# Row DFT one pass later, rows normalised further ahead, nine tiles transposed by DMA, and a new order of the first loads

## The chip, the cores and the metric

The kernel runs on one core of a Trainium2 chip. The metric is the device time of one execution in microseconds (us). One execution was also recorded by the hardware profiler, and the lines shown below come from that record. "SP", "ACT" and "POOL" queues are the DMA queues that these engines issue into; DVE is VectorE, PE is TensorE.

## The reference, cut to what matters

```
xn = layernorm(x, over D)                      # x: 1 x 2048 x 576, bf16
s  = irfft2(rfft2(xn, axes (S, D)) * (w_r + i w_i))
z  = gelu(xn @ w_in)                           # 2048 x 4608
z1, z2 = z[:, :2304], layernorm(z[:, 2304:])
g  = (w_sp @ z2 + b_sp) * z1                   # w_sp: 2048 x 2048
out = x + s * silu(g @ w_out)
```

Every step after the first needs xn, in the 2048 x 576 form with the 576 columns on the partitions (`xnT`): both the row DFT of `rfft2` and the product with `w_in` contract over the columns.

## The kernel before, in words

The 2048 rows are 16 tiles of 128 rows (`MT = 16`, index `m`). The 576 columns are padded to five blocks of 128 (`KS = 5`): four full ones (a row is folded about its middle) and one block that holds the 64 columns left over, each twice.

**The opening stage** goes over the 16 tiles. For a tile, `ln1_stats` and `ln1_aggr` take mean and variance on DVE, `rstd_of` makes the reciprocal deviation on POOL (tile 0: a square root on ACT and a reciprocal on DVE), `ln1_apply` (L293, L296, DVE) writes the normalised row tile into one of three buffers `XN[m % 3]`, `xpose` (L304) transposes its five blocks on PE into PSUM, and ACT copies the result to `xnT` (L305). `p0_fold` (L311, L312, DVE) adds and subtracts the halves, `p0` and `p0_tail` (L329, L321, PE) multiply by the DFT constants `CDSD`, `p0_out` (L334) copies the result on ACT and writes it to the DRAM tensor `Ad` from the POOL queue.

**The chunks** are the other PE work: a `Z2Chunk` (L458) is 128 rows times 384 columns of the second half of `w_in` (five matmuls, the last over 64 partitions), a `Z1Chunk` (L554) 128 columns of the first half times 512 rows. There are 96 of the first and 72 of the second kind; the string `kinds` fixes their order and `fill(n)` puts the next n between the DFT steps, wherever the code calls it. `z2_order` fixes the order of the `Z2Chunk`s: the first eight are tiles 0 to 3 with column chunks 0 and 1, the next eight the same tiles with chunks 2 and 3, the third eight with 4 and 5, and from the 25th on a tile has all its six chunks in a row. Each chunk is evicted by a gelu on ACT (L477, L471, L563), and its statistics are taken on DVE when a running estimate of the load (`spend`, `z2_stats`) leaves room.

PE, DVE and SP follow the order of the code exactly (a manual schedule); ACT and POOL are ordered by the framework. In the loop over `m` from 2, iteration `m` does `p0_fold(m)`, `ln1(m + 3)`, `ln1_apply(m + 2)`, two `fill`s and `p0(m)`; the transposes stand one or two tiles ahead.

**The later stages**: `p1`, `p2`/`p3`, `p4`, `p5` are the other passes of the Fourier filter, with chunks between them; `p1_read` (L342) reads `Ad` back when all tiles are written. The last stage (`main`, from 203 us on) multiplies by `w_sp`: seven products of half size (`prod`, L617) per unit in place of eight, with sums of `Z2` blocks (`tsum`, L601 to L605, DVE) and sums of `w_sp` slabs (`slab_sums`, L540, DVE) as operands. `w_sp` is loaded by DMA transposes (`load_slab`, L534).

**Loads**: each of the DMAs from the SP and ACT queues takes one of eight semaphores in turn, and waits for the DMA that had it eight transfers earlier. So SP, which issues nearly all loads, runs at most about eight transfers ahead.

Of the kernel before, what the change touches and what calls it, by code (L numbers as in the profile page):

```python
# [10 lines left out]
ACT = mybir.ActivationFunctionType  # L11
ALU = mybir.AluOpType
BF16 = mybir.dt.bfloat16
F32 = mybir.dt.float32
P = 128
# [75 lines left out]
def kernel(  # L91
# [135 lines left out]
    HT = H2 - 2 * P  # L227
    wv = B_w_in.rearrange("(a d) f -> a d f", a=2)

    def load_win_main(t, fs, eng=nc.sync):  # L230
        for a in range(2):
            eng.dma_start(out=t[:, a:KS - 1:2, :], in_=wv[a, 0:2 * P, fs].rearrange("(b p) f -> p b f", p=P))

    def load_win_tail(t, fs):
        for q in range(4):
            nc.sync.dma_start(out=t[q * HT:(q + 1) * HT, KS - 1, :], in_=wv[q % 2, 2 * P:H2, fs])

    def load_win(t, fs):
        load_win_main(t, fs)
# [5 lines left out]
        load_win(wb, fs)  # L245

    nc.scalar.dma_start(out=ident[:], in_=cd_id.ap())
    for m0, m1 in ((0, 1), (1, 2), (2, 4)):
        nc.sync.dma_start(out=XC[0][:, m0:m1, :], in_=xv[:, m0:m1, :])
    for n in range(2):  # L250
        load_win_main(WIN2[:, :, n * ZC:(n + 1) * ZC], slice(Fh + n * ZC, Fh + (n + 1) * ZC), nc.scalar)
    for g in range(3):
        (load_win if g else load_win_tail)(WIN2[:, :, 2 * g * ZC:2 * (g + 1) * ZC], slice(Fh + 2 * g * ZC, Fh + 2 * (g + 1) * ZC))
        if g == 0:
            nc.sync.dma_start(out=CDSD, in_=cd_cdsd.ap().rearrange("p (a k l) -> p a k l", a=2, k=3))
        load_x(g + 1)
    nc.sync.dma_start(out=G1, in_=cd_g1.ap().rearrange("p (s k) -> p s k", s=N2))

    def rstd_of(mv, n, tag):
        ve = small.tile([P, n], F32, tag=tag + "v")  # L260
        nc.gpsimd.tensor_scalar(out=ve[:], in0=mv[:, :, 1], scalar1=1e-5, scalar2=one[:, 0:1], op0=ALU.add, op1=ALU.mult)
        rs = small.tile([P, n], F32, tag=tag + "r", bufs=5)
        nc.gpsimd.tensor_tensor(out=rs[:], in0=ve[:], in1=mhalf[:, 0:n], op=ALU.pow)
        return rs
# [7 lines left out]
    def ln1_aggr(m):  # L272
        mv = small.tile([P, 1, 2], F32, tag="mv1", bufs=5, name="mv1")
        nc.vector.bn_aggr(out=mv[:, 0, :], in_=st1[m][:])
        if m == 0:
            rs = small.tile([P, 1], F32, tag="l11r", bufs=5, name="rs1")
            nc.scalar.activation(out=rs[:], in_=mv[:, :, 1], func=ACT.Sqrt, bias=eps[:], scale=1.0)
        else:
            rs = rstd_of(mv, 1, "l11")
        ln1_of[m] = (mv[:, 0, 0:1], rs[:, 0:1])  # L280

    def ln1(m):
        ln1_stats(m)
        ln1_aggr(m)

    st1 = {}
    ln1_of = {}

    def ln1_apply(m):
        xn = XN[m % 3]  # L290
        mean, rs = ln1_of[m]
        xr = XC[m // 4][:, m % 4, :].rearrange("p (a d) -> p a d", a=2)
        nc.vector.tensor_scalar(out=xn[:, 0:4 * P].rearrange("p (b a i) -> p a b i", b=2, a=2),  # L293
                                in0=xr[:, :, 0:2 * P].rearrange("p a (b i) -> p a b i", b=2), scalar1=mean, scalar2=rs,
                                op0=ALU.subtract, op1=ALU.mult)
        nc.vector.tensor_scalar(out=xn[:, 4 * P:KS * P].rearrange("p (r a i) -> p r a i", r=2, a=2),  # L296
                                in0=xr[:, None, :, 2 * P:H2].to_broadcast((P, 2, 2, HT)), scalar1=mean, scalar2=rs,
                                op0=ALU.subtract, op1=ALU.mult)

    def xpose(m):  # L300
        xn = XN[m % 3]
        pt = psh.tile([P, KS, P], BF16, tag="h")
        for ks in range(KS):
            nc.tensor.transpose(pt[:, ks, :], xn[:, ks * P:(ks + 1) * P], ident[:])  # L304
        nc.scalar.activation(out=xnT[:, m, :, :], in_=pt[:], func=ACT.Identity)  # L305

    Adw = Ad[:].rearrange("(c m p) l -> m p c l", c=2, p=P)

    def p0_fold(m):
        xe, xo = xnT[:, m, 0:KS - 1:2, :], xnT[:, m, 1:KS - 1:2, :]  # L310
        nc.vector.tensor_tensor(out=FS[m % 4][:, 0, :, :], in0=xe, in1=xo, op=ALU.add)  # L311
        nc.vector.tensor_tensor(out=FS[m % 4][:, 1, :, :], in0=xe, in1=xo, op=ALU.subtract)  # L312
# [19 lines left out]
    def p0_out(m):  # L332
        sg = PST[m % 8].rearrange("p (c l) -> p c l", c=2)
        nc.scalar.activation(out=sg.rearrange("p c (l a) -> p a c l", a=2),  # L334
                             in_=p0_ps[m][:, :, 0:2 * LE].rearrange("p a (c l) -> p a c l", c=2), func=ACT.Identity)
        nc.gpsimd.dma_start(out=Adw[m], in_=sg[:, :, 0:L])

    rowv = lambda t: t[:].rearrange("(p s) l -> p (s l)", s=N2)
    colv = lambda t: t[:].rearrange("(h p) l -> p h l", p=P)
# [354 lines left out]
    zq = iter(range(MT * NZC))  # L694
    yq = iter(range(FT * 4))
    tick = [0]
    kinds = "2" * 32 + "221" * 11 + "21" * 20 + "221" * 9 + "2111" * 4
    kinds += "2" * (MT * NZC - kinds.count("2")) + "1" * (FT * 4 - kinds.count("1"))
    held = []
    place = [0]  # L700
# [8 lines left out]
    def fill(n, lead=1.2, tails=None, ahead=None):  # L709
        for _ in range(n):  # L710
            i = place[0]
            place[0] += 1
            if i % 4 < 2:
                held.append(chunk(i))
                full(held[-1], True)
            if i % 4 == 1:
                if ahead:
                    ahead()
                done = held[:]
                held[:] = [chunk(i + 1), chunk(i + 2)]  # L720
                assert not tails or n == 1
                for r, c in enumerate(sorted(done + held, key=lambda c: c.wide)):
                    c.mm(KS - 1, slice(r % 2 * KT, (r % 2 + 1) * KT), c in held, c in done)
                if tails:
                    tails()
            elif i % 4 >= 2:
                done = [held.pop(0)]
                full(done[0], False)
            else:
                done = []  # L730
            for c in done:
                if c.wide == ZC:
                    z1_store(None, None)
                tick[0] += 1
                c.post()
            spend(0.82 if kinds[i] == "2" else 1.07)
            z2_stats(lead)

    SP, PE, DVE = mybir.EngineType.SP, mybir.EngineType.PE, mybir.EngineType.DVE
    with tc.manual_schedule(engines={SP, PE, DVE}):  # L740
# [4 lines left out]
        def keep_warm(n):  # L745
            pw = psh.tile([P, 512], F32, tag="h", name="pw")
            for i in range(n):
                nc.tensor.matmul(pw[:], lhsT=warm[:, 0:P], rhs=warm, start=True, stop=True)
# [3 lines left out]
        def p0_pair(m):  # L752
            p0_tail(m, False)
            p0_tail(m + 1, True)
            p0_out(m)

        ln1(0)
        ln1_stats(1, (0,))
        nc.vector.reciprocal(out=ln1_of[0][1], in_=ln1_of[0][1])
        ln1_apply(0)  # L760
        nc.scalar.activation(out=THF[:, 0:1], in_=ln1_of[0][1], func=ACT.Gelu_apprx_tanh)
        xpose(0)
        ln1_stats(1, (1,))
        ln1_aggr(1)
        keep_warm(2)
        fill(1, 0)
        ln1(2)
        ln1_apply(1)
        p0_fold(0)
        ln1_apply(2)  # L770
        ln1(3)
        fill(1, 0, lambda: p0_pair(0), lambda: (xpose(1), p0(0, True), xpose(2)))
        p0_fold(1)
        ln1_apply(3)
        p0(1, False)
        p0_out(1)
        ln1(4)
        fill(1, 0)
        fill(1, 0)
        nc.sync.dma_start(out=MM, in_=cd_mm.ap().rearrange("p (a k) -> p a k", a=3))  # L780
        for m in range(2, MT):
            if m % 2 == 0:
                xpose(m + 1)
            spend(0.78, 2.35 if m + 3 < MT else 0.6)
            p0_fold(m)
            if m + 3 < MT:
                ln1(m + 3)
            if m + 2 < MT:
                ln1_apply(m + 2)
            if m % 2 == 0:  # L790
                fill(1, 0)
                fill(1, 0, lambda: p0_pair(m), lambda: p0(m, True))
            else:
                p0(m, False)
                p0_out(m)
                fill(1, 0)
                if m + 1 < MT:
                    xpose(m + 1)
                fill(1, 0)
            if m in (6, 9):  # L800
                load_win1(m // 9)
        for ch in range(4):
            p1_read(ch)
        load_w(0)
# [15 lines left out]
        for hh in range(0, N2, 2):  # L820
            fill(2)
            if hh + 2 < N2:
                p2(hh + 2)
                spend(0.25, 1.5)
            if hh % 8 != 6:
                fill(1)
            p3(hh)
            spend(0.5)
# [26 lines left out]
        load_z1(0)  # L855
        tick[0] += 4
        z2_stats(99)
        for w in (0, 2, 1):
            tsum(0, w)
        later.append(partial(slab_sums, 2, 0, 2))  # L860
        assert place[0] > kinds.rindex("2")
        nc.sync.dma_start(out=BB, in_=B_b_sp.rearrange("(a s) -> a s", a=1).to_broadcast((P, S)))
# [2 lines left out]
            slab_sums(i, 0, 1)  # L865
        fill(len(kinds) - place[0])
        z1_store(None, None)
        assert not stats_q and not norm_q
        for i in range(2):
            slab_sums(i, 0, 2)  # L870
# [49 lines left out]
```

## Time and profile before

| | |
|---|---|
| median of 7 runs | 499.93 us (499.62 to 500.75) |
| the profiled execution, its own time | 500.48 us |
| its span in the profile | 498.7 us |
| PE busy | 487.8 us, 98% of the span |
| DVE, ACT, POOL busy | 341.0, 169.4, 207.6 us |
| PE clock granted | 1.00 throughout |
| opening stage, from the first transposes to its last row DFT | 5.6 to 48.5 us |
| first `p1` matmul | 59.36 us |
| first product of `main` | 202.82 us |

A line of instructions reads: line of the code, engine, operation, output and input, number, then busy time and mean duration, and then the time that the engine was idle just before and what it waited for. Matmuls are pipelined: a single one is given with some 0.33 us, but eight 128x384 matmuls in a row take 1.30 us in the chain of waits, and five transposes 0.28 us. The working below goes by these.

### The profile page before, as it was taken

To read this page: it belongs to the slowest core of one execution; us is meant where nothing else is said; L and a number is where in the kernel's file an instruction comes from. 1 tells how busy PE (TensorE), PEld (TensorE's weight loads), DVE (VectorE), ACT (ScalarE), POOL (GpSimd) and SP (SyncE) were. 2 spreads that over 40 slices of the span, in tenths; PEclk is the share of its full clock that TensorE was granted. 3 is DMA by queue.
4 is the path that set the end of the run, shared out by engine and by line. 5 is a ranking of instruction groups with operands and counts; after the bars stand their busy time and mean duration, and the time that the engine had idled before them with its cause. 6 is when DMAs were issued, how large, how long until landed. Compare 5 with 4: busy or idle time off the path is not lost.

```text
span 498.7 us, 9373 instructions
## 1 busy us (share of the span) xinstructions
PE 487.8 (98%) x3454; PEld 309.2 (62%) x3454; DVE 341.0 (68%) x747; ACT 169.4 (34%) x355; POOL 207.6 (42%) x280
## 2 busy tenths in 40 slices
PE   6999999999999999899999999999999999999996
PEld 2666454555556544466666677666666678888885
DVE  5776588898656797965565648856666547877634
ACT  4878777686878656200000011100000011000001
POOL 2664223444242684435535400455354311666500
PEclk9999999999999999999999999999999999999999
DMA  7971778988362999672111599021111753111202
GB/s 228 320 209 50 251 264 261 320 228 219 127 248 84 247 222 274 190 249 64 33 46 50 124 165 220 27 61 34 49 47 33 174 135 99 50 45 46 77 27 70
DMA packets 86766, 70.67 MB, mean 142 GB/s; under 512 B 39776, under 2 KB 79328, under 8 KB 86464
## 3 DMA queue, kind: packets, MB, share of 16 engines
q1 hardware_dynamic: 80480, 55.54, 42.3%
q0 software_dynamic: 5008, 13.71, 8.2%
q10 hardware_dynamic: 1232, 0.82, 0.6%
q8 instruction: 27, 0.44, 0.4%
q14 instruction: 19, 0.16, 0.1%
HBM read 40.40 MB, written 21.26 MB: 124 GB/s over the span
## 4 chain that ended last, share of the span: by engine, by line
PE 88%; DVE 3%; ACT 3%; DMA 2%; issue 1%; SPq 0%; POOL 0%; DVEq 0%; ACTq 0%
PE pm L617 43%; PE po L671 13%; PE ph L458 13%; PE ph L554 12%; PE pb L386 2%; PE pa L329 1%; DMA AR<-in_A_x_dram 1%; PE pa L374 1%; PE pa L428 1%; ACT Z L471 1%; DMA AR<-c_cdsd 1%; PE pa L350 1%; PE pa L402 1%; ACT Z L477 1%; PE pt L304 1%
## 5 line engine op out<-in xcount | busy, mean ns | idle before, releaser
L617 PE MATMUL pm<-AR,Z 128*128 128x384 bf16 (+1 forms) x864 | 138.8, 308 | 0.0
L621 DVE TENSOR_TENSOR AR<-pm,AR 128x384 f32<-128x384 f32 (+3 forms) x162 | 82.4, 512 | 70.8 <-PE pm L617 67.0
L617 PEld LDWEIGHTS <-Z 128*128 128x128 bf16 x864 | 84.5, 98 | 40.5
L617 PE MATMUL pm<-AR 128*128 128x384 bf16 (+1 forms) x648 | 107.0, 308 | 2.0 <-DVE AR L540 1.9
L458 PE MATMUL ph<-AR 128*128 128x384 bf16 (+1 forms) x480 | 89.6, 327 | 1.7 <-ACT AR L305 0.9
L554 PE MATMUL ph<-AR 128*128 128x512 bf16 (+1 forms) x360 | 85.9, 379 | 0.0
L617 PEld LDWEIGHTS <-AR 128*128 128x128 bf16 x648 | 63.3, 98 | 32.8 <-DVE AR L540 2.2
L631 ACT ACTIVATE AR<-pm 128x384 f32<-128x384 f32 (+1 forms) x27 | 12.3, 454 | 187.4 <-PE pm L617 187.4
L671 PE MATMUL po<-AR 128*128 128x288 bf16 x540 | 66.6, 286 | 0.0
L671 PEld LDWEIGHTS <-AR 128*128 128x128 bf16 x594 | 56.9, 98 | 13.9
L458 PEld LDWEIGHTS <-AR 128*128 128x128 bf16 (+1 forms) x480 | 40.0, 97 | 37.2 <-issue 14.3
L605 POOL TENSOR_TENSOR AR<-Z,AR 128x1024 bf16<-128x1024 bf16 x26 | 55.3, 2125 | 12.2 <-PE pm L617 12.1
L632 POOL TENSOR_TENSOR AR<-AR 128x384 f32<-128x384 f32 (+1 forms) x27 | 23.0, 852 | 80.4 <-ACT AR L631 75.8
L574 POOL DMA_DIRECT2D Z1d<-AR x55 | 32.0, 582 | 58.5 <-ACT AR L563 54.1
L554 PEld LDWEIGHTS <-AR 128*128 128x128 bf16 (+1 forms) x360 | 30.2, 97 | 28.1 <-issue 5.1
L563 ACT ACTIVATE AR<-ph 128x512 bf16<-128x512 f32 x72 | 42.1, 593 | 15.6 <-PE ph L554 15.4
L477 ACT ACTIVATE Z<-ph 128x384 bf16<-128x384 f32 x66 | 31.9, 500 | 23.4 <-PE ph L458 23.2
L674 ACT ACTIVATE TH<-po 128x576 f32<-128x576 f32 x15 | 9.8, 650 | 77.8 <-PE po L671 77.8
L635 POOL TENSOR_TENSOR AR<-AR 128x384 f32<-128x384 f32 (+1 forms) x27 | 30.0, 1112 | 11.8 <-DVE AR L621 11.8
L485 DVE BATCH_NORM_STATS2 st<-Z 128x6 f32<-128x384 bf16 x66 | 32.5, 544 | 1.5 <-ACT Z L477 1.5
L628 DVE TENSOR_TENSOR AR<-AR 128x384 bf16<-128x384 bf16 (+1 forms) x108 | 31.7, 334 | 0.9
L680 DVE SCALAR_TENSOR_TENSOR AR<-TH,po 128x576 bf16<-128x576 f32 x15 | 11.3, 754 | 30.0 <-ACT TH L674 29.9
(83 smaller groups left out, 474.9 us busy)
## 6 DMA issues: line engine op xcount, KB each, us to landing
Z1d<-AR POOLq DMA_DIRECT2D x55, 128.0 KB, 4.2
AR<-Z1d SPq DMA_DIRECT2D x36, 192.0 KB, 3.0
AR<-in_A_x_dram SPq DMA_DIRECT2D x18, 144.0 KB, 2.8
AR<-in_B_w_out_dram SPq DMA_DIRECT2D x1, 2592.0 KB, 10.7
Ad<-AR POOLq DMA_DIRECT2D x16, 144.5 KB, 4.1
AR<-Ad SPq DMA_DIRECT2D x4, 578.0 KB, 6.0
AR<-in_A_w_r_dram SPq DMA_DIRECT2D x16, 144.5 KB, 4.2
AR<-in_A_w_i_dram SPq DMA_DIRECT2D x16, 144.5 KB, 4.2
```

The costliest lines, as they stand in the source:

```text
L458: nc.tensor.matmul(self.ph[:], lhsT=xnT[rows, self.m, ks, :], rhs=WIN2[rows, ks, n * ZC:(n + 1) * ZC], start=start, stop=stop)
L477: nc.scalar.activation(out=zc, in_=ph[:], func=ACT.Gelu_apprx_tanh)
L485: nc.vector.bn_stats(out=z2s[m][:, n, :], in_=zc)
L554: nc.tensor.matmul(self.ph[:].rearrange("p (a t) -> p a t", a=4), lhsT=wb[rows, ks, (fi % WG) * P:(fi % WG + 1) * P], rhs=xnT[rows, 4 * tq ...
L563: nc.scalar.activation(out=zs, in_=ph[:], func=ACT.Gelu_apprx_tanh)
L574: (nc.sync if place[0] > len(kinds) - 16 else nc.gpsimd).dma_start(out=d, in_=s_)
L605: (nc.gpsimd if u else nc.vector).tensor_tensor(out=t, in0=zblk(p, 1, 0), in1=t2, op=ALU.subtract)
L617: nc.tensor.matmul(dst, lhsT=z[:, s, :], rhs=SLB[SA[name]][:, s, 0:nt], start=(s == 0 and not more), stop=(s == HM - 1), skip_group_check= ...
L621: nc.vector.tensor_tensor(out=out, in0=x, in1=y, op=ALU.add)
L628: nc.vector.tensor_tensor(out=o, in0=o, in1=zb[:, f, h, 0:nt], op=ALU.mult)
L635: nc.gpsimd.tensor_tensor(out=ux, in0=p1a, in1=B[0], op=ALU.add)
L671: nc.tensor.matmul(pv[:, hh, :], lhsT=U[:, fi, h, i * P:(i + 1) * P], rhs=WOUT[:, fi, c0 + hh * H2:c0 + hh * H2 + w // nh], start=(fi == 0 ...
```

## The change

1. **Row DFT one pass later.** The loop over `m` now starts at 0 and four more chunks stand in the opening stage (36 in place of 32); `p0(0)` comes after four chunks and three transposed tiles.
2. **Rows further ahead.** Iteration `m` takes `ln1(m + 5)` and `ln1_apply(m + 4)`.
3. **Tiles 7 to 15 by DMA.** For these, `xpose_dma` (a DMA transpose from the SP queue, SBUF to SBUF, 128 rows by five blocks) stands right behind `ln1_apply`, and replaces the five PE transposes and the ACT copy. Tiles 0 and 1 are copied out of PSUM by DVE instead of ACT.
4. **Two first rows by square root.** Tiles 0 and 1 take the deviation by ACT's square root, whose table is loaded early by a dummy; tiles 2 and 3 have one of the two POOL steps on DVE.
5. **First loads on three queues.** The weights of the first two chunks come before the third row tile, from SP and ACT, and the four small tails from POOL. `CDSD` is loaded after row tile 3. `load_win1` for the `Z1Chunk`s moves from the loop to the front; the constants `G1` (in two halves) and `MM` move from the front into and behind the loop. `Ad` of tiles 11 to 15 is written from SP.
6. **Later on**, two chunks are taken out of the `p3` stage (so before the last `p5` loop the count comes out at 133, where that loop needs no chunks to align), and two of the three first `tsum`s of `main` move behind the first `slab_sums`.

```diff
-    def load_win_main(t, fs, eng=nc.sync):
-        for a in range(2):
+    def load_win_main(t, fs, eng=nc.sync, halves=(0, 1)):
+        for a in halves:
...
     nc.scalar.dma_start(out=ident[:], in_=cd_id.ap())
-    for m0, m1 in ((0, 1), (1, 2), (2, 4)):
-        nc.sync.dma_start(out=XC[0][:, m0:m1, :], in_=xv[:, m0:m1, :])
-    for n in range(2):
-        load_win_main(WIN2[:, :, n * ZC:(n + 1) * ZC], slice(Fh + n * ZC, Fh + (n + 1) * ZC), nc.scalar)
+    load_row(0)
+    load_win_main(*wh[0], nc.scalar, (0,))
+    nc.scalar.activation(out=THF[:, 1:2], in_=eps[:], func=ACT.Sqrt)
+    load_row(1)
+    load_win_main(*wh[0], nc.sync, (1,))
+    load_win_main(*wh[1], nc.sync)
+    load_row(2)
     for g in range(3):
-        (load_win if g else load_win_tail)(WIN2[...], slice(...))
-        if g == 0:
+        third = (WIN2[...], slice(...))
+        if g:
+            load_win(*third)
+        else:
+            load_win_tail(*third, nc.gpsimd)
+            load_row(3)
             nc.sync.dma_start(out=CDSD, ...)
         load_x(g + 1)
-    nc.sync.dma_start(out=G1, ...)
+    for g in range(2):
+        load_win1(g)
...
-        if m == 0:
+        if m < 2:
             rs = small.tile([P, 1], F32, tag="l11r", bufs=5, name="rs1")
             nc.scalar.activation(out=rs[:], in_=mv[:, :, 1], func=ACT.Sqrt, bias=eps[:], scale=1.0)
         else:
-            rs = rstd_of(mv, 1, "l11")
+            rs = rstd_of(mv, 1, "l11", nc.vector if m < 4 else nc.gpsimd)
...
+    DT = 7
+    def xpose_dma(m):
+        nc.sync.dma_start_transpose(out=xnT[:, m, :, :], in_=XN[m % 3].rearrange("p (k i) -> p k i", k=KS))
+
+    def xpose(m, eng=nc.scalar):
...
+        if eng is nc.scalar:
+            nc.scalar.activation(out=xnT[:, m, :, :], in_=pt[:], func=ACT.Identity)
+        else:
+            eng.tensor_copy(out=xnT[:, m, :, :], in_=pt[:])
...
-        nc.gpsimd.dma_start(out=Adw[m], in_=sg[:, :, 0:L])
+        (nc.gpsimd if m < 11 else nc.sync).dma_start(out=Adw[m], in_=sg[:, :, 0:L])
...
-    kinds = "2" * 32 + "221" * 11 + "21" * 20 + "221" * 9 + "2111" * 4
+    kinds = "2" * 36 + "221" * 10 + "21" * 20 + "221" * 8 + "2111" * 4
...
         ln1(0)
         ln1_stats(1, (0,))
-        nc.vector.reciprocal(out=ln1_of[0][1], in_=ln1_of[0][1])
+        ln1_recip(0)
         ln1_apply(0)
-        nc.scalar.activation(out=THF[:, 0:1], in_=ln1_of[0][1], func=ACT.Gelu_apprx_tanh)
-        xpose(0)
         ln1_stats(1, (1,))
         ln1_aggr(1)
+        nc.scalar.activation(out=THF[:, 0:1], in_=ln1_of[1][1], func=ACT.Gelu_apprx_tanh)
+        xpose(0, nc.vector)
+        ln1_recip(1)
+        ln1_apply(1)
         keep_warm(2)
         fill(1, 0)
+        xpose(1, nc.vector)
         ln1(2)
-        ln1_apply(1)
+        ln1(3)
+        fill(1, 0)
         p0_fold(0)
         ln1_apply(2)
-        ln1(3)
-        fill(1, 0, lambda: p0_pair(0), lambda: (xpose(1), p0(0, True), xpose(2)))
-        p0_fold(1)
+        ln1(4)
         ln1_apply(3)
-        p0(1, False)
-        p0_out(1)
-        ln1(4)
-        fill(1, 0)
-        fill(1, 0)
-        nc.sync.dma_start(out=MM, ...)
-        for m in range(2, MT):
-            if m % 2 == 0:
-                xpose(m + 1)
-            spend(0.78, 2.35 if m + 3 < MT else 0.6)
-            p0_fold(m)
-            if m + 3 < MT:
-                ln1(m + 3)
-            if m + 2 < MT:
-                ln1_apply(m + 2)
+        fill(2, 0)
+        xpose(2)
+        p0(0, True)
+        for m in range(MT):
+            if m % 2 == 0 and 0 < m < DT - 3:
+                xpose(m + 3)
+            spend(0.9 if m + 3 < DT else 0.6, 0.5 + 0.6 * (m + 4 < MT) + 1.0 * (m + 5 < MT))
+            if m:
+                p0_fold(m)
+            if m + 5 < MT:
+                ln1(m + 5)
+            if m + 4 < MT:
+                ln1_apply(m + 4)
+                if m + 4 >= DT:
+                    xpose_dma(m + 4)
             if m % 2 == 0:
                 fill(1, 0)
-                fill(1, 0, lambda: p0_pair(m), lambda: p0(m, True))
+                if m == 0:
+                    xpose(3)
+                fill(1, 0, lambda: p0_pair(m), lambda: p0(m, True) if m else None)
             else:
                 p0(m, False)
                 p0_out(m)
                 fill(1, 0)
-                if m + 1 < MT:
-                    xpose(m + 1)
+                if m + 3 < DT:
+                    xpose(m + 3)
                 fill(1, 0)
-            if m in (6, 9):
-                load_win1(m // 9)
+            if m in (9, 11):
+                hf = slice((m - 9) * N2 // 4, (m - 7) * N2 // 4)
+                nc.sync.dma_start(out=G1[:, hf, :], ...)
+        nc.sync.dma_start(out=MM, ...)
...
-            if hh % 8 != 6:
+            if hh % 8 != 6 and hh < 26:
                 fill(1)
...
-        for w in (0, 2, 1):
-            tsum(0, w)
+        tsum(0, 0)
         later.append(partial(slab_sums, 2, 0, 2))
...
             slab_sums(i, 0, 1)
         fill(len(kinds) - place[0])
         z1_store(None, None)
+        for w in (1, 2):
+            tsum(0, w)
```

## The prediction

> **What bounds the kernel now.** I read the page's busy shares first, then the chain of waits, then busy times by stretch over the opening stage, then single lines in order of time.
>
> ```profile
> PE 487.8 (98%) x3454; PEld 309.2 (62%) x3454; DVE 341.0 (68%) x747; ACT 169.4 (34%) x355; POOL 207.6 (42%) x280
> ...
> PE 88%; DVE 3%; ACT 3%; DMA 2%; issue 1%; SPq 0%; POOL 0%; DVEq 0%; ACTq 0%
> ```
>
> PE is busy for 487.8 of 498.7 us and carries 88% of the chain, at full clock throughout. So the change can win in two ways only: by work taken from PE, or out of the 10.9 us in which PE is idle. Where that idle time lies, by stretch (start:end, length, busy us of PE, PEld, DVE, ACT, POOL, then clock, DMA share and GB/s):
>
> ```profile
> 0.00:10.00 10.00, 6.98 (x29) 2.47 (x29) 4.74 (x17) 3.65 (x5) 2.62 (x12) 1.00 0.73 205
> 10.00:20.00 10.00, 9.23 (x82) 5.87 (x80) 7.58 (x28) 7.75 (x15) 5.79 (x12) 1.00 1.06 329
> 20.00:30.00 10.00, 9.84 (x86) 6.10 (x84) 7.59 (x28) 8.26 (x17) 6.32 (x12) 1.00 1.02 301
> ...
> 40.00:50.00 10.00, 9.84 (x82) 6.00 (x80) 6.89 (x22) 8.27 (x18) 4.55 (x7) 1.00 0.20 61
> ...
> 200.00:210.00 10.00, 8.15 (x47) 4.06 (x46) 9.46 (x16) 2.77 (x5) 4.03 (x6) 1.00 0.66 191
> ```
>
> 3.0 us are lost before 10 us, 0.8 in the next 10, 0.16 in each 10 after that, 1.85 at 206. From 20 us the opening stage is PE's, although DVE (76%) and ACT (83%) are not far off.
>
> **1. Transposes taken from PE.** Five transposes are one piece of the chain:
>
> ```profile
> 14.87 0.28 PE pt L304 x5
> 15.15 1.30 PE ph L458 x8
> ```
>
> Nine tiles go: 9 x 0.28 = 2.52 us. As PE is the bound there this is gained in full, if the tiles come in time otherwise (part 4). ACT loses eleven copies of 0.75 us (two of these go to DVE). The bounds are 0 (another engine is the real bound) and 2.52; I take 2.52.
>
> A rule that speaks against this edit is in the Trainium skill, VectorE: DVE Perf Modes, "Rules for kernel authors": transpose 128x128 on TensorE if PSUM will do as the destination, by the DMA crossbar otherwise; it gives 390 ns and 1309 ns. The trace's 0.056 us per transpose is cheaper still than the page has it, but it is paid on the engine that bounds the kernel. By the page's 1309 ns five blocks one after the other would be 6.5 us, an estimate, 0.3 past the round of part 4, and three rounds would lose 0.9.
>
> **2. The opening.** Before, PE starts the chunks at 7.08 and starves:
>
> ```profile
> 7.08 0.34 PE L458 MATMUL ph<-AR 128*128 128x384 bf16 x1 [0.58 <-ACT AR L305]
> 7.69 0.65 PE L458 MATMUL ph<-AR 128*128 128x384 bf16 x3 [0.28 <-DMA AR<-in_B_w_in_dram]
> 8.65 0.34 PE L458 MATMUL ph<-AR 128*128 128x384 bf16 x1 [0.31 <-DMA AR<-in_B_w_in_dram]
> 9.13 0.65 PE L458 MATMUL ph<-AR 128*128 128x384 bf16 x3 [0.15 <-DMA AR<-in_B_w_in_dram]
> ...
> 10.68 0.66 PE L329 MATMUL pa<-AR 128*128 128x290 bf16 x4 [0.40 <-DMA AR<-c_cdsd]
> ...
> 14.71 0.44 PE L304 MATMUL pt<-ident,AR 128*128 128x128 bf16 x5
> ```
>
> Eight matmuls (1.30 us) take until 9.8. Iteration m = 2 begins at 14.71, with four chunks and three tiles transposed. After, iteration 2 begins with eight chunks and five tiles. Four chunks are 16 matmuls of 0.1625 (2.60) and four tails (0.43), two tiles 0.56; so the same point of before is 14.71 + 3.03 + 0.56 = 18.30.
>
> The new chain: row tile 0's statistics end at 4.21 as now (its load stays first). ACT's square root (0.29) started at 4.62 behind its table load; now the table is there, so 4.26 to 4.55. Reciprocal 0.17, apply from 4.80, transposes 5.26 to 5.7. DVE first takes row 1's other half (0.41) and aggregate (0.21), then copies tile 0 out of PSUM. The trace has no such copy; from below 0.41 (512 elements in SBUF, L293), from above 0.84 (L354's 0.76 for 578 elements, scaled to 640); I take 0.8, as a read of PSUM is L354's case: 6.05 to 6.85. The first chunk starts at 6.9. Its weights: up to 1.08 MB of rows and first weights, plus 0.2 MB of tails, lie ahead of the last needed, where before it was 1.6 MB; at the 1.43 MB that had moved by 7.0 they land by about 6.5, so PE does not starve. Chunk 0.65, tile 1 transposed (DVE applies it 7.0 to 7.6), chunk, copy by DVE until 8.65, tails, two chunks: PE runs dry at 10.4. DVE: `ln1(2)`, `ln1(3)` 1.0 each, fold 0.45, apply(2) with its first part done at 11.5: PE waits 1.1 us, then `xpose(2)`, p0(0) 0.6, a wait for ACT's copy of 0.75, chunk from 12.7; tile 3's apply stands behind `ln1(4)` and is done at 13.2 to 13.4, p0(1)'s fold behind `ln1(5)` and apply(4), at 15.2; another 0.5 us of waits, two chunks, tile 4: iteration 2 begins at 17.4. From there DVE needs 0.45 + 0.97 + 0.57 = 2.0 us per tile, PE 2.3, so DVE draws ahead.
>
> Gain 18.30 - 17.4 = 0.9. Bounds: 1.6 with copies of 0.41 and the waits cut to match; -0.8 if row tiles 4 to 7 (2.6 MB down the line, by the rates of before near 11 us, wanted at 11.5) are 1.7 late. Also the 0.16 us waits of each 10 us (p0 for `p0_fold`) should go, as the fold now stands first with its tile long there: +0.3 (0 to 0.5).
>
> The Trainium skill, DMA: Bandwidth & Descriptors, "Rules for kernel authors", says that spreading DMAs over three issuing engines does not add bandwidth, as they share the same 16 DMA engines. The DMA share above is already 1.06 from 10 us on; I took only the order as the gain, and the same rates.
>
> **3. The first products of `main`.**
>
> ```profile
> 203.59 0.69 DVE L603 TENSOR_TENSOR AR<-AR,Z 128x1024 bf16<-128x1024 bf16 x1
> 204.19 3.09 DVE L540 TENSOR_TENSOR AR<-AR 128x1024 bf16<-128x1024 bf16 x5
> ...
> 206.13 1.47 PE L617 MATMUL pm<-AR 128*128 128x384 bf16 x8 [1.85 <-DVE AR L540]
> ```
>
> The second product (P6) waits for three slab sums, which stand behind three `tsum`s. With two of these (0.60 + 0.69) moved behind, it starts 1.3 us earlier. Then the addition of P6 to P1, after which P7 may write the same PSUM bank, stands behind the rest of DVE's queue: 204.67 + two `tsum`s 1.38 + two slab sums 1.24 + 0.56 = 207.85, while PE would come to P7 at 207.36: 0.5 us given back. Net 0.85 (0.4 to 1.4).
>
> **4. What the crossbar costs.** Nearest rows, the `w_sp` transposes of 128 x 1024 from DRAM:
>
> ```profile
> L534 SPq DMA_TRANSPOSE AR<-in_B_w_sp_dram x32: 1237/1307/2913, 160.2 to 406.0; - x32
> ...
> DMA to landing us min/median/max: 3.6/4.6/8.5
> ```
>
> A tile has 5/8 of that. Two deadlines. (a) The buffers: apply(m + 3) overwrites what the transpose of m reads, and stands three iterations behind; at 2.27 us of PE per tile less the 0.57 of the apply, a round may last 6.2 us. By the median the 4.6 fits. What waits behind it on DVE is the fold of the next tile, the next rows' statistics, and with the fold PE. (b) The first one: SP issues tile 7 only when both `load_win1` are issued. Rows, weights and these are 6.5 MB with `CDSD`; before, 6.44 MB had moved by 24 us, so about 24.5 with the first `Ad` writes. Tile 7's DMA then stands behind what is in flight, and lands near 28.5; apply(10) waits for it, and the fold of tile 7 is done near 29.5; PE wants it at 17.4 + 12.1 = 29.5. No margin: I put -0.4 (0 to -7, below).
>
> **5. The rest.** `G1` and `MM` come at 34 us and later, where the DMA share is 0.2 to 0.4, and are wanted at 59: nothing. `Ad` of the last tiles leaves from SP (3.4 us to landing, from `Z1d` writes) rather than POOL (4.1 and 0.75 of issue): `p1_read`, whose cover is eleven chunks, starts sooner; nothing, as PE did not wait for it. Two chunks fewer before `p5`: the last `p4` copy (1.02 us on ACT, right behind the matmuls) then lies under a chunk and tails of 1.13 us: -0.1 (0 to -0.4). DVE gets two copies and two small steps, some 2 us in 341, off the path later on.
>
> **Sum** against the profiled execution's 500.48: 2.52 + 0.9 + 0.3 + 0.85 - 0.4 - 0.1 = 4.07, so 496.4. That execution lay 0.55 above the median of 499.93; on the median's scale 495.9. What this kernel's runs can tell from no change is 0.2%, 1.0 us.
>
> **Rivals.**
> *A, the crossbar round is too long (slower).* One mechanism: three `XN` buffers, in-order DVE. If a transpose takes L from apply to landing, each of the three rounds over tiles 7 to 15 grows by L - 6.2. The 4.07 + 0.4 of the rest are eaten at L = 6.2 + 4.47/3 = 7.7; at 8.5, the longest of the L534 rows, 6.9 us are lost: 499.93 + 6.9 - 4.47 = 502.4. For it: the queue is shared with `G1`, with `Ad`, and the DMA share is over 1 until 28 us. Against: the median of 4.6 for a larger tile was taken in stretches just as full. 0.12.
> *B, the opening gives nothing.* DVE's order (five tiles' statistics before the loop) or late rows cost what the weights give: -0.8 in place of 0.9, sum 2.4, 497.5. For it: PE runs dry twice in my chain, behind DVE. 0.17.
> *C, not PE but ACT and DVE set the pace of the opening stage.* The chain holds a run of ACT and DVE from 17.26 to 22.7; then the transposes gain nothing, sum 1.5, 498.4. Against: both lose or keep work per tile and PE is idle only 0.16 in 10. 0.06.
> *D, C and a mild A together,* within 1 us of before: 0.05.
>
> **How the numbers follow.** The main case has 0.60, and its own range is 494.6 to 497.2 (gain 2.7 to 5.3, by the bounds of copies, `tsum`s and first transpose). B, C and the main case make it faster: 0.60 + 0.17 + 0.05 (C in part) = 0.82, which I lower to 0.79 as part 4 has no margin. Within 0.2%: 0.07. Slower: 0.14, A and a heavier one. The range that holds 8 in 10 leaves out A and the best tenth: 494.4 to 499.0.
>
> **What would show it.** Right: no `pt` transposes past tile 6, PE near 1.3 us per eight chunk matmuls from 7 us on without waits for `in_B_w_in`, iteration 2 at 17 to 18 us, P6's wait under 0.8 us, first `p1` some 0.2 to 1 us earlier in spite of four chunks more ahead of it. Wrong: PE or DVE waiting on the transposes' DMA (A), DVE's statistics waiting for `in_A_x` before 13 us (B), PE idle behind ACT's `Z` evictions with no transposes left (C).

## The result, and the profile after

The changed kernel takes 498.08 us (median of 14 runs, 496.97 to 500.3) against 500.08 for the kernel before (36 runs, 499.4 to 500.94): ratio 0.9963 [0.9955, 0.997]. It is faster by 2.0 us where 4.07 were forecast: the sign was right, the size was not. Its profiled execution takes 497.90 us with a span of 496.1, which is 2.58 under the 500.48 of before; the two profiles exaggerate, as the one of before lay 0.40 above its median and this one 0.18 below. The runs also spread more: these 14 and 12 more (e0, below) reach from 496.97 to 501.9, 5 us, where the 36 runs of before keep within 1.5 and no group of them below exceeds 2.4.

The page, busy shares and shares of the chain:

```profile
PE 486.0 (98%) x3409; PEld 306.9 (62%) x3409; DVE 342.2 (69%) x752; ACT 162.2 (33%) x346; POOL 205.2 (41%) x275
...
PE 87%; DVE 5%; DMA 4%; ACT 2%; POOL 1%; issue 1%; DVEq 0%; ACTq 0%; POOLq 0%
```

PE still bounds the kernel, with 45 instructions and 1.8 us less work (2.45 less than e4 below, which keeps the rest of the change and has the 45 transposes on PE again). DMA's share of the chain went from 2% to 4%. The same stretches as before, and one stretch that was not looked at then, of the changed kernel:

```profile
0.00:10.00 10.00, 8.79 (x41) 3.93 (x42) 6.19 (x22) 4.67 (x9) 3.44 (x13) 1.00 0.85 262
10.00:20.00 10.00, 8.36 (x73) 4.94 (x72) 9.72 (x37) 6.32 (x12) 5.81 (x11) 1.00 1.08 338
20.00:30.00 10.00, 10.00 (x80) 5.99 (x77) 7.65 (x28) 7.54 (x16) 8.13 (x16) 1.00 0.85 195
...
40.00:50.00 10.00, 8.81 (x64) 4.78 (x62) 2.71 (x10) 6.14 (x14) 0.39 (x1) 1.00 1.07 213
...
140.00:160.00 20.00, 18.66 (x169) 11.44 (x168) 10.65 (x16) 15.42 (x33) 5.57 (x13) 1.00 0.53 184
...
200.00:210.00 10.00, 9.21 (x54) 4.94 (x53) 9.93 (x16) 2.13 (x4) 4.35 (x5) 1.00 0.66 183
```

The second-last of these in the kernel before:

```profile
140.00:160.00 20.00, 19.47 (x177) 11.69 (x176) 11.94 (x17) 15.79 (x34) 5.25 (x12) 1.00 0.51 184
```

PE's idle time in the first 20 us went from 3.79 to 2.85, at 20 to 30 from 0.16 to 0.00, at 206 from 1.85 to 0.79. But at 40 to 50 it went from 0.16 to 1.19, with the DMA share at 1.07 where before it was 0.20, and at 140 to 160 from 0.53 to 1.34. The forecast had neither of the last two. PE's lines in order of time show where:

```profile
11.71 0.45 PE L321 MATMUL pt<-ident,AR 128*128 128x128 bf16 x5 [1.34 <-DVE AR L307]
...
17.46 0.44 PE L321 MATMUL pt<-ident,AR 128*128 128x128 bf16 x5
...
46.02 0.67 PE L349 MATMUL pa<-AR 128*128 128x290 bf16 x4 [0.29 <-DVE AR L331]
...
48.01 0.30 PE L341 MATMUL pa<-AR 64*128 64x290 bf16 x2 [0.77 <-DMA AR<-AR]
...
59.80 0.41 PE L370 MATMUL pa<-AR 128*128 128x289 bf16 x2
...
203.20 1.47 PE L637 MATMUL pm<-AR 128*128 128x384 bf16 x8 [0.53 <-ACT AR L651]
```

Iteration 2 begins at 17.46 (0.84 earlier than the equivalent 18.30). At 46.02 PE waits for the fold of tile 14 and at 48.01 for tile 15 itself, which the crossbar has not delivered: 1.06 us. P6, the last line, waits 0.53 instead of 1.85, and no longer for DVE but for ACT. The first `p1` product comes at 59.80. The 59.36 in the table for the kernel before is its start in the chain of waits; in the same view as 59.80 it is

```profile
59.20 0.41 PE L350 MATMUL pa<-AR 128*128 128x289 bf16 x2
```

so it comes 0.60 later, but with four chunks (3.03) more behind it: 2.43 earlier in effect.

SP's own lines say why tiles 14 and 15 are late (start, time on SP, line, count):

```profile
24.54 11.65 SPq L315 DMA_TRANSPOSE AR<-AR  x7
36.24 0.57 SPq L831 DMA_DIRECT2D AR<-c_g  x1
36.90 3.14 SPq L315 DMA_TRANSPOSE AR<-AR  x2
40.13 0.54 SPq L356 DMA_DIRECT2D Ad<-AR  x1
40.72 0.57 SPq L831 DMA_DIRECT2D AR<-c_g  x1
```

The first half of `G1` (512 KB) is issued between tile 13 and tile 14, so the transposes of 14 and 15 stand behind it in the same queue. The line's own view gives what that does to the time from issue to landing:

```profile
L315 SPq DMA_TRANSPOSE AR<-AR x9: 1199/1251/1834, 24.5 to 38.2; - x9
...
DMA to landing us min/median/max: 2.6/4.6/9.8
```

The median of 4.6 is what the forecast worked with; 9.8 is not. The loss at 150 us is on ACT, in order of time:

```profile
147.50 0.48 ACT L491 ACTIVATE Z<-ph 128x384 bf16<-128x384 f32 x1
147.87 0.20 ACT L491 ACTIVATION_READ_ACCUMULATOR Z<-ph 128x1 f32 x1
148.10 0.84 ACT L494 ACTIVATE TH<-Z 128x768 bf16<-128x768 bf16 x1
148.85 0.19 ACT L494 ACTIVATION_READ_ACCUMULATOR TH<-Z 128x1 f32 x1
148.95 1.00 ACT L429 ACTIVATE AR<-pa 128x1024 bf16<-128x1024 f32 x1
```

and PE just after:

```profile
150.00 0.61 PE L422 MATMUL pa<-AR 128*128 128x128 bf16 x8 [0.93 <-ACT AR L429]
```

PE is through with the second `p4` group by about 147.6, but ACT copies it out only from 148.95 on: first it takes the sums and the square of row tile 14 (L491, L494), which this tile does on ACT and not on DVE. PE needs that PSUM bank for the fourth group and waits 0.93 us. The count of chunks ahead of this stage moved by two (four added in front, two left out of `p3`), so tile 14 now ends exactly here.

### The profile page after: what moved, and what is told of

It reads as the page before. It is cut to its first block, busy times and chain, and to the rows that moved or that the text cites. A ratio compares the mean times of both kernels' runs of the same rounds, so it can differ in the third digit from the quotient of the medians.

```text
span 496.1 us, 9307 instructions
## 1 busy us (share of the span) xinstructions
PE 486.0 (98%) x3409; PEld 306.9 (62%) x3409; DVE 342.2 (69%) x752; ACT 162.2 (33%) x346; POOL 205.2 (41%) x275
## 4 chain that ended last, share of the span: by engine, by line
PE 87%; DVE 5%; DMA 4%; ACT 2%; POOL 1%; issue 1%; DVEq 0%; ACTq 0%; POOLq 0%
PE pm L637 43%; PE po L691 13%; PE ph L574 13%; PE ph L478 10%; DMA AR<-AR 3%; PE pb L406 2%; DMA Z1d<-AR 1%; PE pa L448 1%; PE pa L394 1%; PE pw L764 1%; DVE st L283 1%; PE pa L422 1%; PE pa L370 1%; DVE AR L427 0%; DVE AR L307 0%
## 5 line engine op out<-in xcount | busy, mean ns | idle before, releaser
L478 PE MATMUL ph<-AR 128*128 128x384 bf16 (+1 forms) x480 | 87.8, 327 | 0.3 <-ACT AR L323 0.3
L497 ACT ACTIVATE Z<-ph 128x384 bf16<-128x384 f32 x66 | 30.9, 499 | 20.5 <-PE ph L478 20.1
```

The costliest lines, as they stand in the source:

```text
L478: nc.tensor.matmul(self.ph[:], lhsT=xnT[rows, self.m, ks, :], rhs=WIN2[rows, ks, n * ZC:(n + 1) * ZC], start=start, stop=stop)
L497: nc.scalar.activation(out=zc, in_=ph[:], func=ACT.Gelu_apprx_tanh)
```

## The experiments

Each kernel is compared with runs of the kernel before on the same chip: median 499.84 (24 runs) in the first group, 500.05 (24) in the second, 500.2 (17) in the third, 500.13 (9) in the last. The ratio and its interval are given as recorded; the ratio is not always the quotient of the two medians. The letters in the expectations name the theories as they stood when each was written.

**First group: the two places.**

*e0_after_again*, the changed kernel as it is.

> The changed kernel itself, once more, as the measure for its variants on the same chip. Theory and rival both: 498.1, near 2.0 below the kernel before. If the time that the opening stage loses to late transposes differs from execution to execution, its times spread over 2 us or more (before: 1.5), and this profile shows another PE idle time between 40 and 50 us than the 1.19 of the first.

498.93 (12 runs, 497.0 to 501.9), ratio 0.9984 [0.9968, 1.0001]. In this execution PE lost 0.73 us at 20 to 40 us, to tile 7, and 0.89 at 40 to 50, to the last tiles. With the first 14 runs the median of 26 is 498.43. The late arrivals are in the profiles of after, e0 and e2, but not in the same place or of the same size. That fits the spread; no run shows that the spread comes from it.

*e1_g1_behind*, both halves of `G1` behind the transpose of tile 15.

```diff
-            if m in (9, 11):
-                hf = slice((m - 9) * N2 // 4, (m - 7) * N2 // 4)
-                nc.sync.dma_start(out=G1[:, hf, :], ...)
+            if m == 11:
+                for hf in (slice(0, N2 // 2), slice(N2 // 2, N2)):
+                    nc.sync.dma_start(out=G1[:, hf, :], ...)
```

> The changed kernel with both halves of G1 issued behind the transpose of tile 15 (iteration 11) instead of the first half ahead of tiles 14 and 15. Theory Q (tiles 14 and 15 are late because 512 KB of G1 stand ahead of them in SP's queue): both land within 6 us, PE's idle time between 40 and 50 us falls from 1.19 to under 0.4, the time falls by 0.8 to 1.1 (497.1) and spreads less. Rival S (the SBUF to SBUF transposes and the Ad writes are slow by themselves): no change, 498.1, PE idle still about 1.

498.13 (12 runs, 496.43 to 500.26), ratio 0.9961 [0.9948, 0.9974]. The longest landing falls from 9.8 to 6.6 us and PE is not idle from 40 to 50 us:

```profile
40.00:50.00 10.00, 10.00 (x73) 5.91 (x72) 4.77 (x14) 7.15 (x15) 0.83 (x2) 1.00 1.04 222
```

So `G1` ahead of them in the queue is what made tiles 14 and 15 late here: PE lost 1.19, 0.89 and 1.75 us from 40 to 50 us in after, e0 and e2, and nothing in the six profiles with `G1` behind them (e1, both of e3, e6, e7, e10). It does not do so always: e9, below, has `G1` in the same place, all its transposes land within 5.7 us, and PE loses nothing there. The time is 0.8 below e0 of the same group, as expected, but the intervals overlap, and it is only 0.3 below the 498.43. PE is earlier at `p1`, but its transfers are not (SP issues the reads of `Ad` at 54.80, 54.55 in the changed kernel). PE in order of time, in `p1`:

```profile
59.27 0.41 PE L370 MATMUL pa<-AR 128*128 128x289 bf16 x2 [0.48 <-DMA AR<-Ad]
...
69.65 0.41 PE L370 MATMUL pa<-AR 128*128 128x289 bf16 x2 [0.57 <-ACT AR L372]
...
71.53 0.41 PE L370 MATMUL pa<-AR 128*128 128x289 bf16 x2 [0.57 <-DMA AR<-in_A_w_r_dram]
```

1.6 us are given back there in this execution, and tile 7 costs 0.48 more at 20 to 40 us.

*e2_sums_tile13*, tile 13 instead of 14 takes its sums on ACT.

```diff
-    ACT_SUMS = (6, 8, 10, 12, 14)
+    ACT_SUMS = (6, 8, 10, 12, 13)
```

> The changed kernel with the ACT sums taken for tile 13 instead of tile 14. Theory K (the new chunk count puts tile 14's squares on ACT right ahead of the first p4 evictions, PE then waits 0.93 us for the PSUM bank): PE's idle time from 140 to 160 us falls from 1.33 to about 0.5, time down 0.8 (497.3). Rival (any tile's evictions delay p4 there, or the idle time is that of reading Ed): idle stays above 1, no change.

498.24 (7 runs, 495.85 to 498.8), ratio 0.9956 [0.994, 0.9973].

```profile
140.00:160.00 20.00, 19.38 (x170) 11.31 (x168) 10.86 (x16) 14.20 (x28) 5.75 (x14) 1.00 0.54 191
```

PE's idle time here falls from 1.34 to 0.62, by 0.7. Which tile's squares stand ahead of that copy is the cause of the second loss: PE's idle time here is 1.33 or 1.34 in after, e0, e1 and e4 with tile 14, and 0.62 in e2, both of e3, e8 and e10 with tile 13. The same execution, the longest of the seven, lost 2.86 us to late transposes (1.11 at 20 to 40, 1.75 at 40 to 50), so the total says little.

*e3_both*, e1 and e2 together.

> Both edits of the two runs before. If Q and K hold, the gains add as the waits lie in different stages: 1.6 to 1.9 below the changed kernel, 496.3. If one gain is given back in a later stage (p5 and the first w_sp slabs, which wait for PE and the DMA queues), 496.9 or more.

497.27 (6 runs, 496.55 to 499.01), ratio 0.9956 [0.9942, 0.997]; run again in the third group, below, 0.9919, an interval that does not meet this one. The median is 1.7 below e0 of the same group, as expected. In this profile both losses are gone (landing at most 4.7 us, 0.02 idle from 20 to 50 us). Some of it returns at P6:

```profile
202.16 1.47 PE L637 MATMUL pm<-AR 128*128 128x384 bf16 x8 [1.11 <-DVE AR L560]
```

P6 starts 1.04 us earlier than in the changed kernel (202.16 for 203.20). PE is ready for it 1.62 earlier, and waits 1.11 for DVE's slab sums, where the changed kernel waited 0.53 for ACT.

**Second group: what single parts are worth.**

*e4_dt16*, all sixteen tiles transposed by PE.

```diff
-    DT = 7
+    DT = 16
```

> The changed kernel with DT = 16: all 16 tiles transposed on PE, all else kept. It gives back 9 x 0.28 = 2.52 us of PE work and takes away every wait for a crossbar transfer. Theory W (the crossbar pays for itself only in part, since its late arrivals cost PE about 1 to 2 us, more in some executions than in others): 0.5 to 1.5 slower than the changed kernel (499.2 to 500), no PE idle time between 20 and 50 us, and times that spread by 1.5 us or less. Rival X (the crossbar gives its full 2.5 and the time goes elsewhere): 500.6, spread as in the changed kernel.

498.9 (12 runs, 498.43 to 500.25), ratio 0.9977 [0.9966, 0.9987]. PE's busy time is 488.46, 2.45 more than in the changed kernel (2.52 forecast), and from 20 to 50 us it never waits:

```profile
20.00:40.00 20.00, 20.00 (x174) 12.57 (x170) 15.98 (x59) 16.98 (x33) 14.76 (x26) 1.00 0.52 152
40.00:50.00 10.00, 10.00 (x81) 6.20 (x80) 6.55 (x17) 7.86 (x17) 0.72 (x1) 1.00 0.53 113
```

Its median is 1.15 below that of before, where the changed kernel's 26 runs are 1.5 below (498.43 for the 499.94 of all 60 runs of before beside them), and by the intervals the two can't be told apart. So the crossbar, which takes 2.5 us of work from PE, brings some 0.4 us as it is placed, which these runs can't tell from nothing. The three profiles with the unchanged placing (after, e0, e2) lost 1.19, 1.62 and 2.86 us of PE from 20 to 50 us, 1.9 on average: that accounts for most of it.

*e5_tsum_only*, the kernel before with the last part of the change alone (two `tsum`s behind the slab sums).

```diff
-        for w in (0, 2, 1):
-            tsum(0, w)
+        tsum(0, 0)
...
+        for w in (1, 2):
+            tsum(0, w)
```

> The kernel before with one edit: two of the three first tsums of main behind the slab sums. By the prediction 0.85 faster, by the two traces 0.74: 499.2, with PE's wait at the second product 0.5 in place of 1.85. Rival (the queue behind gives it all back at the later products): no change, 499.9.

499.08 (12 runs), ratio 0.9979 [0.9971, 0.9987]: 1.05 us (0.65 to 1.45) for a forecast of 0.85.

```profile
204.29 1.47 PE L617 MATMUL pm<-AR 128*128 128x384 bf16 x8 [0.53 <-ACT AR L631]
```

P6 waits 0.53 as in the changed kernel, and for the addition of its predecessor's result on ACT, no longer for DVE.

*e6_ad_pool*, e3 with all `Ad` writes from POOL, as before the change.

```diff
-        (nc.gpsimd if m < 11 else nc.sync).dma_start(out=Adw[m], ...)
+        nc.gpsimd.dma_start(out=Adw[m], ...)
```

> Both edits of e3_both and Ad of all tiles written from POOL, as in the kernel before. Theory R (the four Ad writes on SP take 8.4 us to landing against 4.4 from POOL and stand behind G1, so the p1 reads start late): p1 reads are issued 1 us or more earlier than the 53.3 to 54.8 us of the runs with SP, p1 matmuls wait for nothing, time 0.3 to 0.8 below e3_both. Rival (SP's writes are late only because p0 is): no change.

502.11 (7 runs, 500.62 to 504.33), ratio 1.003 [1.0015, 1.0045]: the whole change is lost, and the expectation fell. POOL and then PE, in order of time:

```profile
54.11 0.26 POOL L274 TENSOR_SCALAR ve<-mv,one 128x1 f32<-128x1 f32 x1 [7.26 <-DVE mv L521]
54.45 0.56 POOL L276 TENSOR_TENSOR rs<-ve,mhalf 128x1 f32<-128x1 f32 x1
54.97 1.47 POOL L356 DMA_DIRECT2D Ad<-AR  x2
```

```profile
63.51 0.41 PE L370 MATMUL pa<-AR 128*128 128x289 bf16 x2 [3.78 <-DMA AR<-Ad]
```

A small step of the chunks' normalisation stands ahead of the last two `Ad` writes on POOL, and waits 7.26 us for DVE. The writes are issued at 54.97, the reads of `Ad` for `p1` at 59.20 (53.33 in e3), and PE waits 3.78 us. After that the granted clock falls (stretches as before, the clock third from the end):

```profile
62.00:64.00 2.00, 0.49 (x4) 0.32 (x4) 0.00 (x0) 0.05 (x1) 0.00 (x0) 1.00 0.99 395
64.00:66.00 2.00, 2.00 (x8) 0.86 (x7) 0.06 (x1) 1.20 (x2) 0.00 (x0) 0.51 1.01 410
66.00:68.00 2.00, 2.00 (x10) 1.05 (x8) 1.95 (x4) 0.36 (x1) 0.54 (x1) 0.63 1.04 358
68.00:70.00 2.00, 2.00 (x14) 0.91 (x13) 0.81 (x2) 1.74 (x4) 0.83 (x2) 1.00 0.78 225
```

With the clock at 0.51 and 0.63 for 4 us, another 1.7 us of work at full clock are lost (2 x 0.49 + 2 x 0.37).

*e7_xn4*, e6 with a fourth buffer for the normalised rows.

```diff
-    XN = [reg("XN", i * KS * P, KS * P) for i in range(3)]
+    XN = [reg("XN", i * KS * P, KS * P) for i in range(3)] + [reg("TT", 0, KS * P)]
...
-        xn = XN[m % 3]
+        xn = XN[m % 4]
```

> e6_ad_pool with a fourth XN buffer (in a region that is free in the opening stage). Theory A of the prediction (three buffers and the in-order DVE turn a late transfer into a wait): DVE's waits in ln1_apply for the transposes (2.2 to 5.3 us a run) go, and PE's idle time of 0.5 to 1.1 between 20 and 40 us falls by about half, as the fold of tile 7 no longer stands behind an apply that waits for the same transfer; 0.3 to 0.6 faster than e6_ad_pool. Rival (PE waits for the landing of tiles 7, 14 and 15 itself): DVE's waits move to the fold, no change.

503.21 (6 runs), ratio 1.0062 [1.0042, 1.0082]. PE's idle time from 20 to 40 us goes from 1.03 (e6) to 0.00, which fits a wait for the buffer; but other profiles with three buffers and the new first loads show anything from 0.00 to 1.11 there, and the total is ruled by the same wait in `p1` (4.11 us). It settles nothing.

**Third group: the placing, and the first loads.**

*e8_dma_8_to_13*, e2 with only tiles 8 to 13 by crossbar; 7, 14 and 15 by PE, and `G1` where the change has it.

```diff
+    XD = range(8, 14)
...
-                if m + 4 >= DT:
+                if m + 4 in XD:
...
-                if m + 3 < DT:
+                if m + 3 < MT and m + 3 not in XD:
```

> The changed kernel with the sums edit of e2, and the crossbar kept for tiles 8 to 13 only: 7, 14 and 15, whose transfers come late in the profiles, go by PE. Theory Q' (a crossbar tile is worth 0.28 us where its transfer is not awaited, and the losses sit at 7, 14 and 15): PE has under 0.3 us of idle time between 20 and 50 us; against e2 3 x 0.28 = 0.84 is paid and 1.2 to 2.9 no longer lost: 0.5 to 1.5 faster than e2, 497.0 or less, with times that spread by 2 us or less. Rival (any tile by DMA makes waits, as the DMA engines are full): idle time of 1 us or more stays, time as e2 or slower.

496.54 (6 runs, 496.06 to 499.32), ratio 0.9937 [0.9916, 0.9957].

```profile
20.00:40.00 20.00, 20.00 (x155) 12.18 (x154) 15.39 (x59) 15.08 (x31) 14.83 (x26) 1.00 0.89 187
40.00:50.00 10.00, 10.00 (x77) 6.00 (x75) 8.68 (x21) 7.76 (x16) 0.22 (x1) 1.00 0.79 143
```

No idle PE, as Q' has it. With 0.84 us more work on PE (three tiles), the median is 1.7 below that of e2. That fits three tiles that cost more than they save, but e2 ran in another group, the intervals overlap, and e3 alone moved by 1.1 between these two groups. In this group e3 (e3_again, below), which keeps the three tiles on the crossbar with `G1` behind them, is as fast.

*e9_old_loads*, the changed kernel with the first loads in the order and on the queues of before.

```diff
-    load_row(0)
-    load_win_main(*wh[0], nc.scalar, (0,))
+    for m0, m1 in ((0, 1), (1, 2), (2, 4)):
+        nc.sync.dma_start(out=XC[0][:, m0:m1, :], in_=xv[:, m0:m1, :])
+    for w in wh:
+        load_win_main(*w, nc.scalar)
...
-    load_row(1)
-    load_win_main(*wh[0], nc.sync, (1,))
-    load_win_main(*wh[1], nc.sync)
-    load_row(2)
...
-            load_win_tail(*third, nc.gpsimd)
-            load_row(3)
+            load_win_tail(*third)
```

> The changed kernel with the first loads in the order and on the queues of the kernel before (rows 0 to 3 first, four weight loads from ACT, tails and CDSD from SP); all else kept, also the early load_win1. Theory F (of the 0.84 us that the opening gains, most is that the first weights land before the chunks want them): PE waits 0.5 to 1 us for in_B_w_in or CDSD before 12 us again, iteration 2 starts 0.3 to 0.8 later than 17.5 us, time 0.3 to 0.8 above the changed kernel. Rival (the opening's pace is DVE's, the order of loads is hidden): iteration 2 at 17.5, no change.

500.79 (12 runs, 497.55 to 503.13), ratio 1.0008 [0.9985, 1.0031]: all of the gain is gone, though iteration 2 begins only 0.5 us later (17.98). SP holds the rest. Its first transpose, then PE:

```profile
28.01 2.65 SPq L312 DMA_TRANSPOSE AR<-AR  x2
```

```profile
32.92 0.30 PE L338 MATMUL pa<-AR 64*128 64x290 bf16 x2 [3.12 <-DMA AR<-AR]
33.87 0.67 PE L346 MATMUL pa<-AR 128*128 128x290 bf16 x4 [0.65 <-DVE AR L328]
```

```profile
35.00:37.00 2.00, 2.00 (x8) 0.95 (x7) 1.97 (x8) 0.89 (x2) 1.82 (x3) 0.50 0.49 95
```

The transposes start 3.5 us later than in the changed kernel (28.01 for 24.54), as SP is through with the loads later; PE waits 3.12 and 0.65 us for tile 7, and the granted clock then falls to 0.50. Theory F has its 0.5 us in the opening; the rest of the loss it did not foresee. This execution, 503.13, is the longest of the twelve, so it shows the mechanism and not the median's size.

*e3_again*, e3 once more.

> e3_both once more, on the chip of the other two: 497.3, and a ratio to the kernel before of 0.995 with an interval below 0.997. If its gain was chance, it lies at the changed kernel's 498.4.

496.15 (4 runs, 495.3 to 496.84), ratio 0.9919 [0.9904, 0.9934]. Its profile has 0.80 us idle from 20 to 40, now again at tile 7, and none from 40 to 50; P6 waits 0.53 for ACT, not 1.11. Between the two groups the kernel before differs by 0.4 us in its median and e3 by 1.1, the other way. Why is not known, so small differences between groups are not to be trusted, even outside their intervals.

**Last: the version that the runs point to.**

*e10_dt8*, e3 with tile 7 left to PE.

```diff
-    DT = 7
+    DT = 8
```

> e3_both with DT = 8: tile 7 by PE, 8 to 15 by DMA, G1 behind them, sums for tile 13. If the waits at tile 7 (0 to 1 us in the profiles of e3) are what is left of the crossbar's price, PE has under 0.3 us of idle time between 20 and 50 us, 0.28 is paid, and the time is 495.9 or less, spreading by 2 us or less. Rival (the waits move to tile 8): idle time of 0.5 or more stays, time as e3_both, 496.5 to 497.

496.07 (5 runs, 495.73 to 496.46), ratio 0.9914 [0.99, 0.9927]: 4.06 below the kernel before by the medians, and with a spread of 0.7 us. It beats both kernels; e3_again and e8 can't be told from it by their intervals, so what leaving tile 7 to PE is worth is seen in the profile and not in the time.

```profile
20.00:40.00 20.00, 20.00 (x156) 11.98 (x153) 16.25 (x61) 15.09 (x30) 15.16 (x27) 1.00 0.84 189
40.00:50.00 10.00, 10.00 (x73) 5.91 (x72) 8.70 (x20) 7.00 (x15) 0.66 (x1) 1.00 0.77 181
...
140.00:160.00 20.00, 19.38 (x179) 11.61 (x177) 12.41 (x17) 13.60 (x25) 5.71 (x13) 1.00 0.51 179
```

None of the first two stretches is lost, 0.62 of the third (0.53 before the change). Landing takes 4.4 us at most, and the first `p1` comes at 58.47 (59.80 in the changed kernel).

## Why the prediction was right in direction and wrong in size

Its sum, term by term, with what the profiles show:

| term | forecast, us | measured, us | from |
|---|---|---|---|
| transposes off PE | 2.52 | 2.45 | e4 against after, PE busy |
| opening | 0.9 | 0.84 | iteration 2 at 17.46, forecast 17.4 |
| fold waits | 0.3 | 0.3 | 20 to 50 us, but for the tiles below |
| first products of `main` | 0.85 | 0.74 (trace), 1.05 (e5) | output stage 2.35 earlier, `main`'s first product 1.61; e5 |
| crossbar tiles that come late | -0.4 | -1.06 (this trace), -1.2 to -2.9, mean -1.9 | after, e0, e2 |
| two chunks moved | -0.1 | -0.8 | 140 to 160 us; e2 gives 0.7 back |
| sum | 4.07 | 2.5 with -1.06, 1.6 with -1.9 | |

The sum with this trace's -1.06 meets the 2.58 between the profiles; by the -1.9 it is 1.6, and the medians give 2.0, and 1.5 over all 26 runs. The trace agrees with the first four terms. In the opening the chain held too, and not only its end: the first chunk starts at 6.78 (6.9 forecast), PE waits 1.34 us for tile 2 (1.1), and it waits for no weights. One part was off without showing at the end: DVE's copies out of PSUM took 0.49 us, not 0.8.

**The first step that failed** is part 4's -0.4, and behind it a "nothing" in part 5. Part 4 found no margin at the first crossbar tile and priced that one alone. That price was near: tile 7 cost 0, 0.73 and 1.11 us in after, e0 and e2. At the last two tiles, priced at nothing, PE lost 1.19, 0.89 and 1.75 (from 40 to 50 us). Its deadline (a) took the median landing of 4.6 us for every later tile, and the median is indeed 4.6. But part 5 set the move of `G1` at nothing because its bytes are wanted late. What mattered was what stands behind it: SP issues in the order of the code, and tiles 14 and 15, behind 512 KB, are wanted at once. e1 shows it at that place. Of the two ends of the range, 0 to -7, the value near 0 was taken, while L534's row showed a maximum of 8.5.

**The second** is part 5's -0.1 for the chunk count. It looked at the last `p4` copy, and not at what a shift by two places puts in front of the first ones; which tiles do their sums on ACT was in the code. It cost 0.8, and e2 shows it.

**Another "nothing" was right only as long as that part of the change was there**: `Ad` from SP. Part 5 argued that PE did not wait for `p1_read`. With POOL's order kept, it does, for 3.8 us and some 5 to 6 us of time (e6 against e3's two groups). This edit does not win time; it pays for the new order.

**The rivals.** A had the right resource, transposes in a shared queue, and its sign, PE waiting on their DMA, did appear. Its mechanism, a round that grows, did not: PE waits for none of tiles 8 to 13, and tiles 14 and 15 have no later tile that wants their buffer. The waits sit at the two ends of the sequence, the first tile behind the loads and the last behind `G1`. Whether the three buffers have a part in tile 7's wait is open. B is refuted by iteration 2 at 17.46, C by PE's 10.00 of 10 us from 20 to 30. Of the signs of being right one failed: the first `p1` product, forecast 0.2 to 1 us earlier, came 0.60 later. The forecast that DVE would draw ahead held wherever no transfer was late. That the edits are worth about 4 us was borne out only where the two side effects are mended: e3_again and e10 are 4.05 and 4.06 below before by the medians. In e10, with tile 7 given back, the waits of tiles 7, 14 and 15 are 0, PE keeps 0.28 us of work, and P6's wait is 0.94 instead of 0.53.

**Open.** How much of tile 7's wait is the backlog of DMA behind the loads, and how much the fold that stands behind the next apply on DVE: e7 was to tell, and was covered by the wait in `p1`. Why `G1` ahead of tiles 14 and 15 cost nothing in e9, and why e3 differs between its groups. Nor was it tried to move DVE's slab sums, at which P6 waits 0.9 to 1.1 us in three profiles where PE comes earlier (the first of e3, e8, e10).

## What to carry to other kernels

A transfer moved within a queue is priced by the work behind it, not by when its own bytes are wanted: before calling such a move free, list what is issued next in the queue and when that is needed. Work taken off the bound engine is gained only for the items whose replacement comes in time, so look at the first and the last items of a sequence, which meet the loads ahead and the constants behind, and either leave them where they were (e8) or move what they meet (e3). Which of the two is better these runs don't tell. A change of a count shifts every fixed pattern after it, so look at what the shift puts in front of each copy that PE waits for.

## What the runs showed of the hardware

A wait of PE does not only cost its own length. In stretches of 2 us the granted clock was 0.51 and 0.63 after a wait of 3.78 us (e6), 0.50, 0.50 and 0.63 from the end of a wait of 4.11 us on (e7), and 0.88, 0.50 and 0.77 after waits of 3.12 and 0.65 us (e9); after the waits of 1.34 us and less in the changed kernel it stayed at 1.00. In e9 sixteen chunk matmuls then took 4.44 us instead of 2.76.

The Trainium skill, TensorE: Matmul & The Clock Gate, Part 1, says that the clock is halved after an idle window of some 3.4 us and comes back after as long a busy one, the window running freely; 3.78 and 4.11 us agree. In e9 3.12 us with 0.65 close behind was followed by it too, and no run here has 3.12 us alone.

Transposes within SBUF weigh on the DMA engines more than their bytes say: from 20 to 50 us the DMA share is 0.93 at 184 GB/s in the changed kernel and 0.52 at 139 GB/s in e4, where PE does them. So 45 GB/s more come with 0.41 more of share, where e4's 139 take 0.52. Landing took 2.6 to 9.8 us in the changed kernel for the same 128 x 640 tile, and 2.6 to 4.4 in e10.
